# A new written-out order of steps for an attention and mixture kernel on one core: loads first, sums shared between GpSimd and VectorE

## The chip, the cores and the metric

The kernel runs on one core of one Trainium2 chip. The metric is the device time of one execution in microseconds (us); less is better. Before the change the median of three runs is 213.99 us (213.4 to 214.45).

A core has engines that run in parallel, each with its own queue that it works through strictly in order: TensorE (PE, matrix products; PEld is its weight load), VectorE (DVE), ScalarE (ACT), GpSimd (POOL) and SyncE (SP, which here only issues DMAs). An instruction at the head of a queue that waits holds up everything behind it on that engine.

## The reference

```python
scores = scale * np.matmul(x, state.transpose(0, 1, 3, 2))     # 8 batches, 8 heads, 512 tokens, 32 states, 64 deep
a = softmax(scores)                                            # over the 32 states
xread = np.matmul(a, state)
scores2 = scale * np.matmul(state, x.transpose(0, 1, 3, 2))
a2 = softmax(scores2)                                          # over the 512 tokens
sread = np.matmul(a2, x)
attn = np.concatenate([xread, sread], axis=2)                  # 544 rows a head
x = attn.transpose(0, 2, 1, 3).reshape(B * 544, 512)
h = x @ w_in                                                   # 512 to 2048
g = np.maximum(h, 0.0) + alpha * np.minimum(h, 0.0)
return g @ w_out                                               # 2048 to 512
```

`softmax` stands for the reference's three lines (subtract the maximum, exponential, divide by the sum). Inputs and output are float32; inside, the kernel works in float16 with float32 accumulation.

## The kernel before

The whole program is a list of some 1,100 short tokens, the string `ORDER`. A table `steps` maps the first part of a token to a small function, the rest are its arguments; the tokens are issued from first to last, each engine receives its instructions in that order, and the framework adds the waits that the data need. There is no scheduler behind it: the string is the schedule. An argument `a`, `v` or `p` names the engine (ScalarE, VectorE, GpSimd) where there is a choice, and a last number is the PSUM bank that a result takes.

Batches are numbered 0 to 7; "batch 8" is the block of all state rows (8 times 32). For a batch the path is:

1. Loads. `lx.b` loads a batch's tokens (GpSimd's queue, float32 cast to float16 by the DMA, line 157). Batch 0 is loaded as float32 in two halves by SyncE's queue (line 167) and cast by `cx.j.g.e` (line 173; j is the half, g the group of heads). `wi.f` and `wo.i` load quarters of `w_in` and `w_out` (lines 194 and 200), `lst` the states of batches 1 to 7 (line 188); the states of batch 0 come by ScalarE's queue as float32 and are cast by `stc` (line 237). All loads on GpSimd's queue cost GpSimd an instruction each, and stand in its order with its arithmetic.
2. Transposes. `xt`/`xo` (TensorE, and a copy out of PSUM) or `xd` (a transposing DMA) for the tokens; `stt`, `sto`, `sbd`, `str`, `sro` for the states.
3. Scores `sc`, and for batch 0 `tsc` (the scores by token, which the first softmax takes). Softmax over states: `smax`, `ssh`, `sexp`, `ssum`, `snorm`, then `at`/`ao` for batch 0 or `wb` for the others. Softmax over tokens: `tm`, `nb`, `te`, `tsum`, and `tn` (line 436), which scales the exponentials on GpSimd; then `tt` and `rd`, `rdo` for the states' reads.
4. `m.b.f` multiplies the batch's states by a quarter of `w_in`, `mo` takes the product out of PSUM. So `F.b.jc` (line 533, two matmuls of 512 columns) gets `h` for 128 of the 2048 hidden features straight from the softmax weights. `N` (line 586, ScalarE) makes the negative part and `G` (line 589, VectorE) puts `g` together. The first four features' tiles of batch 0 go in halves by `f`, `n`, `g` (lines 555, 570, 574).
5. Batches 0 and 1: `S.b.q.i` (line 603) multiplies two of the 16 feature tiles of `g` by `w_out`, `O` takes the result out. Batches 2 to 8 take a scheme with seven instead of eight products of half matrices: `U.b.i.c` (line 670) forms sums and differences of halves of `g`, each over 128 x 1024 elements (128 x 512 for batch 8), `W.i.c` (line 646) those of `w_out`, once; `P` (line 691) are the products (four matmuls of 256 columns), `K` (line 707) and `Q` (lines 722, 724) take them out. All `U` and `W` run on GpSimd.

`Z.k.n` issues n matmuls of zeros into bank k (line 220). Nothing reads them; they keep TensorE occupied while data are awaited.

In the first 30 us VectorE runs `smax.0.0` (line 363, waiting for `tsc`), the rest of batch 0's softmax, casts and copies, the first `g`, batch 1's `tm` and `sb`, then `G.0.6`, `G.0.5`; TensorE's `F` and `S` of batch 0 follow these.

Of the kernel before, what the change touches and what calls it, by code (L numbers as in the profile page):

```python
# [32 lines left out]
sc.2 tt.1 sb.2 F.1.11.0 tm.2 rdo.0.a smax.2 F.1.13.2 S.0.0.5 mo.2.2.a.1 S.0.0.7 mo.2.2.a.0 N.1.13 G.1.13 N.1.11
O.0.0.a S.0.3.0.5 G.1.11 nb.2.a te.2.1 S.0.3.7 lx.3 S.0.3.2 F.1.15.3 te.2.0 N.1.15 S.0.3.5 G.1.15 F.1.12.1 F.1.6.2
N.1.12 G.1.12 S.0.3.6 N.1.6 S.0.3.3 G.1.6 S.0.2.7 m.3.3.0.3 mo.3.3.v.1 xd.3 ssh.p.2 sexp.2 ssum.2 mo.3.3.a.0 m.3.2
mo.3.2.a F.1.14.1 W.4.0.p S.1.0.6.2 S.0.3.1 N.1.14 G.1.14 F.1.7.0 O.0.2.a N.1.7 G.1.7 S.1.0.4 F.1.3.3 N.1.3 tsum.2
S.0.3.4 S.1.0.0 m.2.3.4.1 O.0.3.a mo.2.3.v.1 mo.2.3.a.0 m.2.1 mo.2.1.a rd.1.0 m.3.0.5.4 mo.3.0.a.0 S.1.0.3 mo.3.0.a.1
S.1.0.5 sc.3 m.4.0.1.5 mo.4.0.a.0 G.1.3 mo.4.0.a.1 W.3.1.p snorm.p.2 wb.2 lx.4 S.1.3.6.3 F.2.3.4 F.2.2.1 F.2.0.5
S.1.0.7 N.2.3 sb.3 tm.3 G.2.3 rdo.1.a smax.3 N.2.2 G.2.2 N.2.0 S.1.0.1 F.2.8.0 S.1.3.7 W.4.1.p tn.2.1 tn.2.0 ssh.p.3
G.2.0 nb.3.a te.3.0 F.2.1.4 N.2.1 S.1.3.1 te.3.1 tsum.3 G.2.1 S.1.0.2 S.1.3.2 tt.2 N.2.8 G.2.8 O.1.0.a F.2.6.1 N.2.6  # L40
G.2.6 S.1.3.0 F.2.14.5 N.2.14 G.2.14 S.1.1.2.4 F.2.9.2 N.2.9 G.2.9 F.2.10.0 N.2.10 G.2.10 rd.2.1 sexp.3 ssum.3 m.3.1
F.2.5.5 mo.3.1.a F.2.11.2 S.1.3.4 S.1.3.3 S.1.2.1.0 S.1.1.3 N.2.11 G.2.11 rdo.2.a U.2.3.0.p N.2.5 xd.4 G.2.5 S.1.2.5
m.4.1.1.2 mo.4.1.a.1 sc.4 tm.4 S.1.3.5 O.1.3.a tn.3.1 F.2.4.5 tn.3.0 F.2.7.2 mo.4.1.a.0 F.2.13.3 N.2.13 lx.5 sb.4
G.2.13 S.1.1.5 tt.3 F.2.12.1 S.1.1.6 S.1.2.7 F.2.15.3 S.1.2.4 smax.4 S.1.2.3 nb.4.a te.4.0 N.2.4 N.2.7 N.2.12 G.2.4
N.2.15 S.1.2.6 S.1.2.2 S.1.1.0 G.2.7 te.4.1 S.1.2.0 O.1.2.a G.2.15 m.4.3 G.2.12 mo.4.3.a m.5.0.5.2 rd.3.3 rdo.3.a
mo.5.0.v.1 xd.5 m.4.2.1.0 mo.4.2.a.0 snorm.p.3 U.2.1.0.p U.2.2.0.p U.2.4.0.p wb.3 S.1.1.1 S.1.1.7 tsum.4 ssh.p.4
S.1.1.4 F.3.9.2 F.3.7.3 mo.5.0.v.0 sexp.4 lx.6 P.2.1.1.1.1 mo.4.2.v.1 N.3.7 O.1.1.a ssum.4 P.2.1.0.0 N.3.9 G.3.7
# [10 lines left out]
N.4.12 G.4.3 P.3.1.1.0 smax.5 F.4.14.4 K.3.1.a N.4.14 G.4.12 U.3.1.0.p U.3.2.0.p P.3.7.0.1.0 U.3.3.0.p G.4.14
P.3.7.1.1 P.3.6.0.0 F.4.15.1 N.4.15 G.4.15 P.3.6.0.1 P.3.6.1.1 N.4.10 G.4.10 P.3.6.1.0 K.3.2.a F.4.8.5 N.4.8 G.4.8
F.4.13.4 N.4.13 G.4.13 P.3.5.1.1 P.3.5.1.0 P.3.5.0.0 m.5.1 mo.5.1.a m.6.2.1.2 mo.6.2.v.0 m.7.3.5.4 mo.7.3.v.0  # L60
P.3.7.1.0 P.3.7.0.0 sc.6 mo.7.3.a.1 mo.6.2.v.1 sb.6 m.6.1.1.5 rd.4.4 mo.6.1.a.0 rdo.4.a m.7.2.2.1 mo.7.2.a.1 U.3.4.0.p
U.4.3.1.p ssh.p.5 U.4.1.0.p U.4.2.0.p smax.6 P.3.5.0.1 P.4.1.1.0.4 K.3.4.a Q.3.1.1 P.3.2.0.0.1 P.4.1.1.1 sexp.5
P.3.3.1.0 P.3.2.0.1 P.3.4.0.1 ssh.p.6 sexp.6 U.4.1.1.p U.4.2.1.p P.3.4.1.0 tm.6 mo.7.2.v.0 P.4.1.0.1 P.3.2.1.1
P.3.2.1.0 Q.3.0.0 P.4.2.0.0.2 P.4.1.0.0 K.4.1.a P.3.4.0.0 P.4.7.0.1.1 P.4.6.0.0 P.4.6.1.0 P.3.3.0.1 P.3.4.1.1
P.4.6.1.1 P.4.6.0.1 ssum.6 P.4.2.1.0 snorm.p.6 P.4.2.0.1 P.3.3.1.1 ssum.5 snorm.p.5 Q.3.1.0 K.4.2.a P.4.5.1.1
P.4.5.0.0 nb.6.a P.3.3.0.0 te.6.1 te.6.0 wb.6 F.6.3.0 wb.5 mo.6.1.a.1 Q.3.0.1.a P.4.2.1.1 P.4.5.0.1 Q.4.0.0 N.6.3
G.6.3 U.4.3.0.p F.5.8.5 N.5.8 G.5.8 tsum.6 F.5.3.3 N.5.3 F.5.2.2 N.5.2 G.5.3 lx.7 F.5.7.0 N.5.7 G.5.2 G.5.7 P.4.5.1.0
# [32 lines left out]
def kernel(  # L100
# [134 lines left out]
    def first_states_cast():  # L235
        live["st0"] = consts.tile([128, 2, D], F16, name="st0")
        nc.gpsimd.tensor_copy(live["st0"], st0_32)
# [538 lines left out]
```

## Time and profile before

| what | value |
|---|---|
| median of 3 runs | 213.99 us (213.4 to 214.45) |
| the profiled execution's own time | 213.49 us |
| its span, first to last instruction | 211.7 us |
| granted TensorE clock, mean share of full speed | 0.997 |
| first 27 us: TensorE's last wait ends | 27.11 us |
| last matmul ends | 207.9 us |
| `G` (line 589), 128x512 | 124 instructions, 85.8 us on VectorE |
| `N` (line 586), 128x512 | 124 instructions, 69.1 us on ScalarE |
| `U` (line 670), 128x1024 | 48 instructions, 2.13 us each on GpSimd |
| `tn` (line 436), 128x512 | 16 instructions, 0.69 us each on GpSimd |

The profile lists each engine's busy time, instructions grouped by source line with their mean duration, what ended an engine's idle time, and busy time within chosen stretches of the span. A busy TensorE is one with a matmul in its pipeline. "POOL 0.98" in a stretch means that GpSimd was busy for 0.98 us of it; DMA shares are the mean use of the 16 DMA engines and can pass 1, since transfers overlap.

### The profile page before, as it was taken

The page shows a single profiled execution, that of the slowest core. Times are in us where ns is not written, and L with a number is a line of the kernel's source. Part 1 is how long each engine was busy: PE and PEld are TensorE (multiplying, and loading weights), DVE is VectorE, ACT ScalarE, POOL GpSimd, SP SyncE. Part 2 cuts the span into 40 slices and gives each one's busy share as a digit, 9 for nine tenths or more (in the row PEclk, how much of TensorE's full clock was granted, in tenths as well). Part 3 has the DMA queues.
Part 4 walks back from the last instruction along what each step waited for, and adds up shares of the span by engine and source line. Part 5 has one row for each costly group of instructions (what it writes and reads, how often), then busy time and mean ns, then how long its engine had stood idle before and what let it go on. Part 6 is the DMA issues. An engine that isn't in the chain of part 4 may idle for free.

```text
span 211.7 us, 4977 instructions
## 1 busy us (share of the span) xinstructions
PE 202.8 (96%) x1979; PEld 133.1 (63%) x1979; DVE 173.0 (82%) x259; ACT 144.0 (68%) x280; POOL 182.0 (86%) x119
## 2 busy tenths in 40 slices
...
GB/s 167 159 193 206 207 196 193 88 136 143 174 144 151 170 82 168 82 3 105 60 185 3 50 62 139 116 247 37 54 99 50 104 0 0 3 96 77 89 86 151
DMA packets 52439, 23.68 MB, mean 112 GB/s; under 512 B 38465, under 2 KB 51393, under 8 KB 52417
## 3 DMA queue, kind: packets, MB, share of 16 engines
...
q8 instruction: 15, 0.25, 0.5%
...
q14 instruction: 8, 0.06, 0.1%
HBM read 17.31 MB, written 8.91 MB: 124 GB/s over the span
## 4 chain that ended last, share of the span: by engine, by line
PE 90%; DVE 5%; DMA 2%; issue 0%; ACT 0%; POOL 0%; DVEq 0%
PE h L533 25%; PE px L691 21%; PE o L603 13%; PE pv L691 11%; PE py L691 5%; PE m_ps L484 4%; PE h L542 3%; PE z L220 3%; PE sr_ps L457 2%; DMA st<-in_state_dram 2%; DVE g L574 2%; PE sc L299 1%; PE xT_ps L284 1%; PE st_ps L231 1%; DVE g L589 1%; DVE m L508 1%
## 5 line engine op out<-in xcount | busy, mean ns | idle before, releaser
L589 DVE SCALAR_TENSOR_TENSOR g<-neg,oma_sb,h 128x512 f16<-128x512 f32 (+1 forms) x140 | 92.8, 709 | 8.0 <-ACT neg L586 6.1
L586 ACT ACTIVATE neg<-h 128x512 f32<-128x512 f32 (+1 forms) x140 | 74.6, 579 | 24.7 <-PE h L533 14.7
L533 PE MATMUL h<-aT,m 128*128 128x512 f16 x248 | 66.2, 379 | 0.2 <-DVE g L589 0.2
L691 PEld LDWEIGHTS <-gsum 128*128 128x128 f16 x416 | 40.4, 98 | 9.8 <-issue 0.7
L533 PEld LDWEIGHTS <-m 128*128 128x128 f16 x248 | 23.6, 98 | 20.8 <-issue 1.9
L691 PEld LDWEIGHTS <-g 128*128 128x128 f16 x312 | 30.5, 98 | 7.8
L603 PE MATMUL o<-w_out_sb,g 128*128 128x512 f16 x128 | 33.2, 379 | 1.1 <-DVE g L574 1.1
L670 POOL TENSOR_TENSOR gsum<-g,g 128x1024 f16<-128x1024 f16 (+1 forms) x14 | 27.8, 1988 | 1.6 <-DVE g L589 0.8
L670 POOL TENSOR_TENSOR gsum<-gsum,g 128x1024 f16<-128x1024 f16 (+1 forms) x14 | 27.8, 1988 | 0.9
L670 POOL TENSOR_TENSOR gsum<-g 128x1024 f16<-128x1024 f16 (+1 forms) x14 | 27.8, 1990 | 0.3 <-DVE g L589 0.2
L670 POOL TENSOR_TENSOR gsum<-g,gsum 128x1024 f16<-128x1024 f16 (+1 forms) x14 | 27.7, 1990 | 0.3
L691 PE MATMUL px<-ws,gsum 128*128 128x256 f16 x208 | 27.1, 273 | 0.0
L603 PEld LDWEIGHTS <-g 128*128 128x128 f16 x128 | 11.9, 98 | 16.6 <-issue 1.8
L707 ACT COPY kept<-px 128x512 f32<-128x512 f32 (+1 forms) x15 | 8.4, 561 | 20.2 <-PE px L691 20.2
L385 POOL TENSOR_TENSOR an<-ts,r 128x1024 f16<-128x1024 f32 (+1 forms) x9 | 15.4, 1720 | 5.5 <-DVE r L382 4.0
L368 POOL TENSOR_TENSOR ts<-ts,mx 128x1024 f32<-128x1024 f32 x7 | 13.4, 1911 | 6.9 <-DVE mx L363 6.9
L510 ACT CAST m<-m_ps 128x512 f16<-128x512 f32 x28 | 15.6, 596 | 3.3 <-PE m_ps L484 3.1
L724 DVE TENSOR_TENSOR oq<-pv,kept 128x512 f32<-128x512 f32 (+1 forms) x14 | 9.0, 645 | 10.2 <-PE pv L691 5.7
L691 PE MATMUL pv<-ws,gsum 128*128 128x256 f16 x104 | 15.0, 273 | 0.0
L691 PE MATMUL px<-w_out_sb,g 128*128 128x256 f16 x104 | 14.8, 273 | 0.0
L691 PE MATMUL px<-w_out_sb,gsum 128*128 128x256 f16 x104 | 14.5, 273 | 0.0
L691 PE MATMUL py<-w_out_sb,g 128*128 128x256 f16 x104 | 14.5, 273 | 0.0
...
## 6 DMA issues: line engine op xcount, KB each, us to landing
...
```

Source lines behind the costliest of these rows:

```text
L368: engine(e).tensor_tensor(blocks(cols(live["ts", b], j, S)), blocks(scored(b, j)), over_blocks(cols(live["mx", b], j, S // N)), ALU.subtract,)
L385: engine(e).tensor_tensor(blocks(cols(live["an", b], j, S)), blocks(cols(live["ts", b], j, S)), over_blocks(cols(live["r1", b], j, S // N) ...
L484: nc.tensor.matmul(t[N * k : N * (k + 1), :], st_head(b, h)[64 * r : 64 * r + 64, :], w_in_sb[64 * r : 64 * r + 64, c, 512 * f : 512 * (f ...
L510: copier(e)(m_tile(b, f)[:, g, :], t[g])
L533: nc.tensor.matmul(h.rearrange("p (r j s) -> p r j s", r=2, j=2), ms[b, f][:, g, 128 * j : 128 * (j + 1)], weights(b, g), start=(g == 0), ...
L586: nc.scalar.activation(neg, h, RELU, bias=0.0, scale=-1.0)
L589: nc.vector.scalar_tensor_tensor(g_tile(b, jc), negs.pop((b, jc)), oma_sb[:, jc : jc + 1], hs.pop((b, jc)), ALU.mult, ALU.add,)
L603: nc.tensor.matmul(outs[b, q], g_tile(b, jc)[:, 128 * q : 128 * (q + 1)], w_out_sb[:, jc, :], start=not begun and jc == 2 * jc2, stop=left ...
L670: engine(e).tensor_tensor(t, x(), y(), op)
L691: nc.tensor.matmul(pbanks[b, name][:, i, :], of(b, c)[:, j, 128 * i : 128 * (i + 1)], moving[:, 4 * c + j, :], start=not begun and j == 0, ...
L707: copier(e)(t, pbanks[b, "x"])
L724: nc.vector.tensor_tensor(osb, pbanks[b, name], kept[b, add], ALU.add)
```

## The change

The order is written anew from the first token to the last. The arithmetic is the same but for the matmuls of zeros. What differs in what is issued:

| tokens | before | after |
|---|---|---|
| matmuls of zeros | 51 in 7 groups | 30 in 10 groups of 3, 18 of them ahead of everything else on TensorE |
| `stc` (first states' cast) | GpSimd | ScalarE |
| `U` on GpSimd / VectorE | 56 / 0 | 39 / 17 |
| `W` on GpSimd / VectorE | 8 / 0 | 7 / 1 |
| `tn` on GpSimd / ScalarE | 16 / 0 | 11 / 5 |
| `mo` on ScalarE / VectorE | 40 / 11 | 46 / 5 |
| `cx` on ScalarE / VectorE | 3 / 1 | 2 / 2 |
| `rdo` on ScalarE / VectorE | 8 / 0 | 5 / 3 |
| `K`, `Q`, `O` taken out by VectorE, where there is a choice | 8 | 9 |

The 18 sums that VectorE takes are, in order, W.1.0, U.2.1.1, U.3.3.0, U.4.1.1, U.6.3.1, U.6.4.0, U.6.4.1, U.7.3.1, U.7.1.1, U.7.3.0, U.7.2.0, U.8.3.1, U.7.4.1, U.8.1.1, U.8.2.0, U.8.2.1, U.8.3.0, U.8.4.1. (A `U.4.2.1` stays on GpSimd.) The code outside the order:

```diff
-    def first_states_cast():
+    def first_states_cast(e):
         live["st0"] = consts.tile([128, 2, D], F16, name="st0")
-        nc.gpsimd.tensor_copy(live["st0"], st0_32)
+        copier(e)(live["st0"], st0_32)
...
     def token_scores(j, g, k=None):
-        if g == 0:
+        if ("tsc", j) not in live:
...
-    def token_norm(b, g):
+    def token_norm(b, g, e):
         e2 = live["e2", b][:, g, :, :]
-        nc.gpsimd.tensor_scalar(
-            e2, e2, live["r2", b][:, g : g + 1], 1.0, ALU.mult, ALU.mult
-        )
+        r2 = live["r2", b][:, g : g + 1]
+        if e == "a":
+            nc.scalar.mul(e2, e2, r2)
+        else:
+            nc.gpsimd.tensor_scalar(e2, e2, r2, 1.0, ALU.mult, ALU.mult)
```

The beginning of the order, up to where batch 0's first layer is under way (the rest is rewritten in the same way):

```diff
-Z.0.9 cx.0.1.a stc stt.0 sbd.0.v Z.1.5 xt.0.0.1.1 cx.0.0.a xt.0.0.0.2 Z.3.6 sto.v cx.1.0.v sbd.1.a xt.0.1.0.3
-xo.0.0.0.v tsc.0.0.4 xo.0.0.1.a cx.1.1.a tsc.0.1 xt.0.1.1.5 smax.0.0 wi.0 xo.0.1.0.a lst ssh.v.0.0 sc.0.0 xo.0.1.1.a
-tsc.1.0.0 Z.1.2 tsc.1.1 sc.0.1 smax.0.1 ssh.v.0.1 lx.1 wi.1 sexp.0.0 wo.0 wi.2 Z.1.5 m.0.0.1.2 tm.0 wi.3 Z.3.11
-mo.0.0.a.1 ssum.0.0 str.1.3 str.0.5 mo.0.0.a.0 Z.4.13 sexp.0.1 ssum.0.1 snorm.p.0.0 at.0.4 sro.1.v xt.1.1.1.0
-xo.1.1.1.v xt.1.1.0.2 xt.1.0.1.1 snorm.p.0.1 at.1.3 nb.0.a te.0.0 te.0.1 sro.0.a m.1.0 xo.1.1.0.a ao.0.v m.2.0.5.0
-f.0.1.0.4 ao.1.a f.0.0.1.2 xt.1.0.0.3 wo.1 mo.2.0.a.1 xo.1.0.1.v mo.1.0.v oma n.0.1.0 g.0.1.0.1 wo.2 n.0.0.1
-xo.1.0.0.v m.1.1 mo.1.1.a m.0.1.1.0 f.0.1.1.3 sc.1 mo.0.1.a.0 mo.0.1.a.1 g.0.0.1.0 g.0.0.1.1 mo.2.0.a.0 f.0.0.0.2
-n.0.0.0 tsum.0 tn.0.0 F.0.5.1 n.0.1.1 g.0.1.0.0 S.0.2.1.4 N.0.5 tm.1 F.0.7.0 nb.1.a sb.1 g.0.1.1.1 F.0.6.5 te.1.1
-te.1.0 g.0.1.1.0 S.0.1.1.3 tn.0.1 g.0.0.0.0 N.0.6 g.0.0.0.1 smax.1 G.0.6 G.0.5 S.0.1.0 m.0.2 mo.0.2.a N.0.7 S.0.2.0
...
+stc.a lst Z.0.3 Z.0.3 Z.0.3 Z.0.3 Z.0.3 Z.0.3 cx.0.1.v stt.0 sto.v Z.1.3 cx.0.0.a xt.0.0.0.1 xo.0.0.0.a cx.1.1.a Z.2.3
+xt.0.0.1.2 sbd.1.v lx.1 Z.3.3 sbd.0.v tsc.0.0.3 cx.1.0.v xt.0.1.0.4 xo.0.0.1.v tsc.0.1 xt.0.1.1.5 str.0.0 xo.0.1.1.a
+Z.1.3 tsc.1.1.1 xo.0.1.0.v sc.0.1 tsc.1.0 str.1.2 sc.0.0 xt.1.0.0.4 wi.0 wi.1 smax.0.0 ssh.v.0.0 sexp.0.0 smax.0.1
+ssh.v.0.1 sro.0.a xt.1.1.0.5 sexp.0.1 xt.1.0.1.3 wo.0 xt.1.1.1.0 xo.1.0.0.a xo.1.1.1.a tm.0 nb.0.a te.0.1 wo.1
+ssum.0.1 snorm.p.0.1 sro.1.v te.0.0 m.0.0.1.4 mo.0.0.v.1 xo.1.1.0.a mo.0.0.a.0 ssum.0.0 snorm.p.0.0 at.1.0 ao.1.a
+m.2.0.2.4 m.1.0 mo.2.0.v.0 xo.1.0.1.v f.0.0.1.5 mo.1.0.a oma n.0.0.1 tsum.0 tn.0.0.p f.0.1.1.1 n.0.1.1 at.0.0 m.1.1
+mo.1.1.a m.0.1.2.3 mo.0.1.a.0 mo.0.1.a.1 g.0.0.1.0 ao.0.v f.0.0.0.0 g.0.1.1.1 g.0.1.1.0 g.0.0.1.1 sc.1 S.0.1.1.1
+F.0.7.2 mo.2.0.a.1 F.0.6.5 S.0.3.0.3 S.0.1.0 N.0.7 wi.2 f.0.1.0.4 sb.1 tm.1 N.0.6 n.0.0.0 G.0.6 nb.1.a S.0.3.1 te.1.1
+g.0.0.0.0 g.0.0.0.1 F.0.4.5 F.0.5.0 G.0.7 S.0.1.3 te.1.0 S.0.2.3.2 S.0.3.3 m.0.2 smax.1 N.0.4 S.0.2.0 G.0.4 wi.3 N.0.5
+n.0.1.0 G.0.5 S.0.3.2 g.0.1.0.1 g.0.1.0.0 W.1.0.v mo.0.2.a F.0.8.5 N.0.8 G.0.8 wo.2 wo.3 F.0.10.0 N.0.10 F.0.9.4
+G.0.10 N.0.9 G.0.9 m.0.3 mo.0.3.a S.0.2.1 F.0.11.5 S.0.2.2 S.0.1.2 F.0.14.0 ssh.p.1 sexp.1 F.0.15.4 S.0.2.4
...
```

On GpSimd the order before is: the first states' cast, then `wi.0`, `lst`, `lx.1`, `wi.1`, `wo.0`, `wi.2`, `wi.3`, then the first arithmetic. After: `lst`, `lx.1`, `wi.0`, `wi.1`, `wo.0`, `wo.1`, with nothing to wait for ahead of them; then `snorm.0.1`, `snorm.0.0`, `tn.0.0`, and behind these `wi.2`, `wi.3`, `wo.2`, `wo.3`.

More of the change, by code (lines that the diff above doesn't have):

```diff
@@ L33 @@
[L33 to L47, printed above, removed]
@@ L58 @@
[L58 to L67, printed above, removed]
@@ L73 @@
-P.5.1.0.0 m.7.1.5.3 mo.7.1.a.0 mo.7.1.a.1 sc.7 U.5.3.0.p sb.7 rd.6.4 rdo.6.a rd.5.0 rdo.5.a P.5.2.1.1.5 F.6.15.3
-N.6.15 tm.7 nb.7.a F.6.11.4 P.4.4.0.1 te.7.0 te.7.1 N.6.11 G.6.15 Q.4.1.0 P.5.2.1.0 P.5.2.0.0 tsum.7 P.5.1.0.1 K.5.1.a
-F.6.13.0 G.6.11 P.5.2.0.1 F.6.12.3 smax.7 P.5.7.0.1.1 N.6.12 G.6.12 F.6.8.4 N.6.8 U.5.1.1.p U.5.2.1.p P.5.6.1.1 N.6.13
-G.6.8 P.5.6.0.1 P.5.7.1.1 G.6.13 U.5.1.0.p U.5.2.0.p P.5.6.0.0 P.5.7.1.0 tn.7.0 ssh.p.7 sexp.7 Q.5.0.0 F.6.0.3
-P.5.6.1.0 F.6.4.4 F.6.9.0 P.5.7.0.0 tn.7.1 K.5.2.v P.5.5.1.0 ssum.7 P.5.5.0.0 N.6.0 U.5.4.0.p N.6.9 G.6.9 P.5.5.1.1
@@ new lines @@
+F.0.7.2 mo.2.0.a.1 F.0.6.5 S.0.3.0.3 S.0.1.0 N.0.7 wi.2 f.0.1.0.4 sb.1 tm.1 N.0.6 n.0.0.0 G.0.6 nb.1.a S.0.3.1 te.1.1
+g.0.0.0.0 g.0.0.0.1 F.0.4.5 F.0.5.0 G.0.7 S.0.1.3 te.1.0 S.0.2.3.2 S.0.3.3 m.0.2 smax.1 N.0.4 S.0.2.0 G.0.4 wi.3 N.0.5
+n.0.1.0 G.0.5 S.0.3.2 g.0.1.0.1 g.0.1.0.0 W.1.0.v mo.0.2.a F.0.8.5 N.0.8 G.0.8 wo.2 wo.3 F.0.10.0 N.0.10 F.0.9.4
+G.0.10 N.0.9 G.0.9 m.0.3 mo.0.3.a S.0.2.1 F.0.11.5 N.0.11 S.0.2.2 S.0.1.2 F.0.14.0 ssh.p.1 sexp.1 F.0.15.4 S.0.2.4
+N.0.14 G.0.11 S.0.3.5 tsum.1 m.1.2 ssum.1 lx.2 snorm.p.1 tn.1.1.p tn.1.0.p N.0.15 S.0.2.5 G.0.14 W.1.1.p W.2.1.p
@@ new lines @@
+te.2.1 te.2.0 F.1.0.1 N.1.0 tsum.2 S.0.0.4 G.1.1 ssh.p.2 G.1.0 sexp.2 S.0.0.6 m.3.0.4.3 m.3.2 F.1.8.0 F.1.15.1
+mo.3.2.a tn.2.0.p mo.3.0.v.0 S.0.0.2 tn.2.1.p mo.3.0.a.1 tt.2 S.1.0.1 ssum.2 N.1.8 G.1.8 F.1.12.4 N.1.12 G.1.12
+S.1.0.0 N.1.15 F.1.13.3 S.1.0.5 G.1.15 N.1.13 G.1.13 S.1.0.4 m.2.1 rd.2.0 rdo.2.v O.0.0.a mo.2.1.a m.2.3.4.1
+mo.2.3.a.1 mo.2.3.a.0 rd.1.2 m.3.3.3.0 mo.3.3.a.1 sc.3 S.1.1.0.1 S.1.1.3 snorm.p.2 W.4.0.p lx.4 wb.2 F.2.7.4 rdo.1.a
+N.2.7 F.2.8.0 N.2.8 sb.3 xd.4 S.1.1.5 F.2.2.2 smax.3 W.3.1.p ssh.p.3 mo.3.3.a.0 tm.3 S.1.0.6 S.1.0.7 O.1.0.a N.2.2
@@ new lines @@
+N.2.6 tn.3.0.p F.2.5.1 G.2.6 N.2.5 F.3.12.0 U.2.3.0.p F.3.3.3 N.3.12 U.2.1.0.p mo.4.1.a.0 N.3.3 tm.4 nb.4.a te.4.0
+S.1.3.1 S.1.3.6 U.2.2.0.p P.2.1.1.0.2 S.1.3.2 G.2.5 P.2.1.0.0 G.3.12 F.2.13.4 tt.3 lx.5 N.2.13 te.4.1 S.1.3.3 S.1.3.0
+O.1.3.a P.2.1.1.1 smax.4 G.3.3 F.3.2.1 N.3.2 m.5.2 G.2.13 m.4.2.0.5 mo.4.2.a.0 rd.3.3 rdo.3.a mo.4.2.a.1 G.3.2
+P.2.1.0.1 K.2.1.v F.3.7.4 U.2.1.1.v N.3.7 G.3.7 F.3.5.0 N.3.5 xd.5 F.3.14.1 ssh.p.4 sexp.4 P.2.2.0.0.3 tsum.4 N.3.14
+F.3.0.5 G.3.5 P.2.6.0.0 ssum.4 P.2.2.0.1 G.3.14 F.3.4.4 P.2.2.1.0 N.3.0 mo.5.2.a N.3.4 G.3.4 G.3.0 F.3.11.0 N.3.11
@@ new lines @@
+F.4.15.0 N.4.3 G.4.3 P.3.6.1.1 N.4.15 G.4.15 sexp.5 P.3.6.0.0 K.3.2.a ssum.5 m.6.1.2.5 m.5.1 mo.5.1.a P.3.7.1.0.3
+P.3.7.0.0 F.4.6.4 N.4.6 G.4.6 F.4.4.0 N.4.4 G.4.4 mo.6.1.a.0 P.3.5.0.0 P.3.5.1.0 P.3.5.1.1 P.3.5.0.1 snorm.p.5
+mo.6.1.a.1 sc.6 tm.6 m.6.2.4.2 mo.6.2.a.1 K.3.4.a m.7.3.5.0 P.3.7.0.1 P.3.7.1.1 sb.6 F.4.12.2 P.3.3.1.0 N.4.12
+P.3.3.0.0 mo.6.2.a.0 P.3.3.1.1 P.3.3.0.1 Q.3.0.1.a Q.3.1.1 P.3.4.1.1 mo.7.3.a.0 wb.5 nb.6.a G.4.12 P.3.4.0.0 U.4.1.0.p
+U.4.2.0.p U.4.1.1.v U.4.2.1.p xd.7 F.5.5.4 F.5.7.1 N.5.7 P.4.1.0.0.5 smax.6 ssh.p.6 tn.5.0.a P.3.4.0.1 P.4.2.0.0.2
```

91 lines of the change are left out of this document (52 added, 39 removed).

## The prediction

> **What bounds the kernel now.** I read the page's busy times first, then who waited on TensorE, then busy times by stretch, last the timeline of the first 28 us.
>
> ```profile
> span 211.7 us, 4977 instructions
> PE 202.8 (96%) x1979; PEld 133.1 (63%) x1979; DVE 173.0 (82%) x259; ACT 144.0 (68%) x280; POOL 182.0 (86%) x119
> ```
>
> TensorE fills 96% of the span. Its waits (total, times, longest):
>
> ```profile
> PE st_ps L231 <- POOL st L237: 1.8, 1, 1.8
> PE z L220 <- DVE zero L214: 1.3, 1, 1.3
> PE o L603 <- DVE g L574: 1.1, 1, 1.1
> PE h L555 <- DVE xT L289: 0.4, 1, 0.4
> PE h L533 <- DVE g L589: 0.2, 1, 0.2
> ```
>
> All are in the first 27.2 us. Busy us by stretch, TensorE to GpSimd:
>
> ```profile
> 30.00:80.00 50.00, 50.00 (x482) 22.18 (x481) 48.15 (x66) 43.81 (x85) 43.40 (x28) 1.00 0.94 144
> 80.00:130.00 50.00, 50.00 (x497) 36.13 (x496) 44.88 (x62) 36.51 (x69) 48.67 (x26) 1.00 0.36 79
> 130.00:180.00 50.00, 50.00 (x464) 35.32 (x463) 46.43 (x72) 35.10 (x72) 47.96 (x29) 1.00 0.39 85
> 180.00:208.00 28.00, 27.91 (x256) 24.76 (x254) 11.75 (x22) 6.01 (x15) 24.95 (x16) 1.00 0.23 76
> ```
>
> From 30 us to the last matmul TensorE never pauses, although GpSimd is at 97% from 80 to 130. So relieving GpSimd gains nothing there by itself. What can be gained lies ahead of 27 us, and what can be lost is TensorE's unbroken run. Ahead of 27 us:
>
> ```profile
> 6.61 1.17 POOL L157 DMA_DIRECT2D xg<-in_x_dram  x1
> 6.87 1.16 DVE L173 CAST xg<-x 128x512 f16<-128x512 f32 x1 [0.73 <-DMA x<-in_x_dram]
> 9.84 0.69 DVE L363 TENSOR_REDUCE mx<-tsc 128x16 f32<-128x512 f32 x1 [1.48 <-PE tsc L337]
> 14.64 1.59 PE L220 MATMUL z<-zero 128*128 128x256 f16 x13
> 19.40 0.48 DVE L574 SCALAR_TENSOR_TENSOR g<-neg,oma_sb,h 128x256 f16<-128x256 f32 x1
> 26.33 0.73 DVE L589 SCALAR_TENSOR_TENSOR g<-neg,oma_sb,h 128x512 f16<-128x512 f32 x1
> 27.11 0.59 PE L533 MATMUL h<-aT,m 128*128 128x512 f16 x2 [0.21 <-DVE g L589]
> ```
>
> VectorE starts the softmax at 9.84, works almost without a gap, ends `G.0.6` at 27.06, and TensorE's last wait is for it (27.11). So the end is set by when VectorE reaches `G.0.6`; behind it TensorE runs 180.8 us to 207.9, and 3.8 us follow for the last copy and store. I compare where the new order has VectorE at points with the same work behind.
>
> **The change, part by part.**
>
> *Work ahead of G.0.6.* By the two orders TensorE has the same real work in front of `G.0.6` but for two tokens each way (`F.0.5`, `S.0.2.1` against `S.0.3.0`, `S.0.1.0`), each two matmuls of 512 columns. So at `G.0.6` what is left is the same, and an earlier `G.0.6` moves the end one for one.
>
> *Zero matmuls.* Of 51, 30 stay. The first nine took 2.10 us, 0.23 each; 18 take 4.2, from 1.33 to 5.5, and the first states' transposes began at 5.19: at most 0.3 late, hidden behind batch 0's tokens, which landed at 5.36 and 6.87. The other 12 (0.12 to 0.24 each, 1.4 to 2.9) stand where TensorE waits for copies. The 13 at 14.64, which reached past the first `an`, are gone. Price zero: VectorE's queue covers them; without that cover, at most 2.9 lost.
>
> *States' cast.* On GpSimd 0.29 at 4.85; on ScalarE the nearest copy took 0.37 (line 249), and ScalarE was idle until 5.36. Zero, bounds -0.1 to 0.3.
>
> *Loads at once.* GpSimd's first load was issued at 5.09, behind that cast; now `lst` and `lx.1` go out at about 1.3, as soon as the identity is made, and `wi.0`, `wi.1`, `wo.0`, `wo.1` follow at 0.55 to 1.2 each. Nothing at 27 us waited for them, so the gain is nil; the cost is that they share the DMA engines with batch 0's tokens, which had these alone:
>
> ```profile
> 3.00:4.00 1.00, 0.43 (x3) 0.00 (x0) 0.00 (x0) 0.00 (x0) 0.00 (x0) 1.00 0.94 267
> 5.00:6.00 1.00, 0.81 (x7) 0.52 (x8) 0.34 (x2) 0.64 (x2) 1.00 (x2) 1.00 1.20 294
> 8.00:9.00 1.00, 1.00 (x6) 0.61 (x5) 0.36 (x2) 0.58 (x2) 1.00 (x2) 1.00 1.28 196
> ```
>
> The last columns are DMA share and GB/s written. GpSimd's loads write 196 GB/s, thus read 392 as they cast. `wi.0`, issued at 5.09, shows in the DMA rate about two us later, so `lst` should flow from 3, when about 0.88 MB of the tokens' 1.05 is still to come. If both share evenly, 0.88 MB of reads go between: 0.88/0.39 = 2.2 us, the second half lands at 9.1 instead of 6.87. Bounds: no delay (6.9); all of `lst` and `lx.1` first, 0.74 MB written at 200 GB/s, 3.7 us (10.5). I take 9.1, for the shares stand near the full 16 engines already.
>
> *From the tokens to the softmax.* VectorE then does `cx.1.0` and two transposes' copies before `smax.0.0`. The cast took 1.16 on VectorE while GpSimd issued a load (6.61 to 7.78; it ended 0.25 after it), 0.62 on ScalarE. GpSimd's issues are over by about 6.5 now, so 0.6 (bounds 0.3 to 1.16), two copies 0.42 each, 0.15 for TensorE's score: start at 10.7, against 9.84.
>
> *From the softmax to G.0.6.* Start-to-start steps of VectorE: four halves of `smax`/`ssh` 2.71, `tm` 1.13, `ssum` 0.86, `sro` 1.08, `mo` 0.62, `ssum` 0.86, `mo` 0.62, `xo` 0.36, two small ones 0.27: 8.5. Next is `g.0.0.1.0`, which needs ScalarE: from 1.4 after the start 0.64 `sexp`, 1.06 `sro`, 0.64, two `xo` 1.18, 0.2, `te` 1.76, `xo` 0.59, `mo` 0.60, `ao` 0.59, `mo.1.0` 1.0, `n` 0.62, less some 0.06 overlap each: 9.6. So VectorE waits 1.1. Then four `g` and an `ao` 1.96, `sb` and `tm` 2.29, `G.0.6` 0.67: 14.5 after the start, 25.2. Before it was 17.2 after its start (two more `mo`, `xo` and four more `g` and `smax.1` stood ahead). Lead: 27.06 - 25.2 = 1.9 us.
>
> *The next tight point* is `F.0.11`, whose bank `G.0.8` frees: 0.80 `g`, 0.67, `smax.1` 1.13, 1.34, 0.80, `W.1.0` 0.7, 0.67, thus 20.6 after the start, 31.3. TensorE has 12 more `F` and `S` (0.432) and two `m` (0.28) behind it there, 5.7 us, than before at `G.0.5` (27.7): 33.4 by before's pace. Lead 2.1, so `G.0.6` decides.
>
> *wi.2 and wi.3* now wait on GpSimd behind `snorm` and `tn`: issued at about 20.1 and 20.9. An unqueued quarter lands in 5.8, the next 2.5 later: 25.9 and 28.5. `m.0.3` is due at about 29.6. Zero, with 1 us to spare; its cover gone, one for one.
>
> *Sums on VectorE.* Twelve of 128x1024 and six of half that: 15 full ones. No row before has VectorE in such a sum. Float16 copies (0.272 for 256, 0.416 for 512) grow 0.56 ns an element: 0.70. Float32 ones (0.424, 0.69): 1.22. The other moves (six `mo` off, `rdo`, `Q`, `cx` on) come to about -1. VectorE's total: 173 - 1 + 15 x 0.7 = 182; at 1.22, 190. Four full ones fall before about 130 us, where VectorE idles 7.0 of the 100 us from 30; eleven later, where it idles 19.8 of 78. Below 1.7 each they are hidden there; I take 0.7, as it is nearest in type, and price zero, with one exception counted above (`W.1.0`).
>
> The clearest case against it is GpSimd's own work: if a VectorE sum must wait for a running one, it waits up to 2.13. The Trainium skill, page "SBUF — State Buffer", section "Who interferes with whom", says that a VectorE instruction with two SBUF inputs contends with a GpSimd one that reads SBUF, and that the later blocks for the whole of the other. The cast above, which ended just behind GpSimd's issue, looks like such a block; of sums no run here shows it yet.
>
> *tn on ScalarE*, 0.69 on GpSimd, at most that on ScalarE, which is at 68%: zero.
>
> **Sum.** -1.9 from `G.0.6`, +0.1 for the 0.3 of first transposes that may show: -1.8. The profiled execution was 213.49, so 211.7; the median is 0.5 above it: 212.2.
>
> **Rivals.**
>
> 1. Tokens hardly delayed (7.5): softmax at 9.1, lead 3.5, the median 210.5. For it: shares above 1 show transfers overlapping. Against: both streams read at 300 to 390 GB/s alone.
> 2. Tokens delayed to the bound, 10.5: softmax at 12.1, lead 0.5, thus no change, 213.5. For it: `lx.1` is cut into pieces as small as the tokens'.
> 3. Slower: VectorE's sums wait for GpSimd's. GpSimd falls to about 146 us busy (69%), a mean wait of 0.69 x 1.07 = 0.73, a sum then 1.4, still hidden. At 2.1 each, four cost 8.4 against 7.0 and eleven 23.1 against 19.8: 4.7 lost, less 1.8: +2.9, 216.9. It decides from about 1.9 each. For it: GpSimd's sums stand back to back, and `G`'s of the next tiles queue behind a waiting sum. Against: after 180 us VectorE is 42% busy, and half of the sums fall near there.
>
> **How the numbers follow.** Forecast 0.37 (own range 211.2 to 213.0), rival 1 0.11, rival 2 0.22, rival 3 0.30 with worse delays of the start in it. What a measurement here can tell from no change is about 0.5%, 1.1 us. Faster 0.47, same 0.22, slower 0.31. The range reaches from rival 1 to rival 3: 210.2 to 217.0.
>
> **What would show it.** Right: the tokens' second cast at 8.5 to 9.5, `smax.0.0` at 10 to 11.3, `G.0.6` done by 25.5, no TensorE wait beyond 0.3 after 32 us, `U` on VectorE near 0.7. Wrong: TensorE waits on line 592's `g` between 30 and 150, `U` on VectorE above 1.7, or `m.0.3` waiting for `wi.3`.

## The result, and the profile after

Each kernel was run 18 times, in turn on one chip. The kernel before took 213.56 us (median; 212.88 to 214.45), the changed one 216.45 us (214.35 to 218.1): ratio 1.011, 95% interval 1.0082 to 1.0138. The change makes the kernel 1.1% slower; forecast was 212.2. The ratios leave out executions more than 1.5% above the fastest of their kernel and are not quotients of the medians (that would be 1.0135 here).

The runs of the changed kernel fall into two groups, 7 from 214.35 to 215.42 and 11 from 216.12 to 218.1. The profiled execution took 217.11 and belongs to the second. Its span and busy times, from the page (engine, busy us, share, instructions):

```profile
span 215.3 us, 4942 instructions
PE 204.7 (95%) x1958; PEld 132.3 (61%) x1958; DVE 180.8 (84%) x276; ACT 148.2 (69%) x287; POOL 147.9 (69%) x95
```

GpSimd lost 34 us of work and VectorE gained 8, as intended and as forecast (182 and "about 146"). The time is elsewhere. The waits of TensorE (engine, what waited, what for; total us, times, longest):

```profile
PE sr_ps L460 <- DMA e2T<-e: 1.8, 1, 1.8
PE at_ps L350 <- POOL an L386: 1.7, 1, 1.7
PE z L221 <- DVE zero L215: 1.3, 1, 1.3
PE m_ps L487 <- ACT xT L290: 0.6, 1, 0.6
PE sc L300 <- ACT m L511: 0.4, 1, 0.4
PE h L536 <- DVE g L577: 0.2, 1, 0.2
```

The first line is new: that wait ends at 59.8 us, where TensorE never paused before. No line names a sum. Busy us by stretch, in the columns of the prediction:

```profile
15.00:20.00 5.00, 2.74 (x33) 0.99 (x32) 4.91 (x9) 4.68 (x12) 1.72 (x2) 0.81 1.24 206
30.00:80.00 50.00, 48.04 (x435) 20.89 (x434) 45.27 (x64) 42.86 (x81) 36.23 (x24) 1.00 0.80 135
80.00:130.00 50.00, 49.95 (x512) 34.13 (x511) 47.05 (x67) 41.67 (x81) 46.90 (x26) 1.00 0.72 118
130.00:180.00 50.00, 50.00 (x487) 36.73 (x485) 46.58 (x73) 36.49 (x75) 43.40 (x23) 1.00 0.23 62
```

From 30 to 80 us 1.96 of TensorE's time is missing; from 80 on it is as full as before, although VectorE now does the sums.

To place the loss I use one curve below: at a point of the trace, the time so far less the real matmuls done so far, each at its undisturbed pace of the trace before (0.2155 us for 512 columns, 0.109 for 256). Both kernels do 189.9 us of such work; the rest is "lost".

| lost by | 28 us | 45 us | 58 us | 60 us | 100 us | the last matmul |
|---|---|---|---|---|---|---|
| before | 15.48 | 16.06 | 16.40 | 16.40 | 16.86 | 17.82 |
| after | 16.43 | 17.51 | 17.87 | 19.96 | 20.70 | 21.42 |

Of 3.6 us, 0.95 are lost by 28 us, 0.5 more by 45 (what takes these was not traced), and 2.1 between 58 and 60; 1.8 of these 2.1 are the wait that ends at 59.8.

The start, in order of time (start, duration, engine, line, what, how many):

```profile
2.59 3.83 PE L221 MATMUL z<-zero 128*128 128x256 f16 x13
6.57 0.42 PE L232 MATMUL st_ps<-ident,st 128*64 128x128 f16 x4
6.92 0.82 PE L221 MATMUL z<-zero 128*128 128x256 f16 x3
```

The states had been cast at 4.87. TensorE still worked through its 18 matmuls of zeros until 6.4, so the first transposes came at 6.57 (before 5.19), and between the next ones stood groups of three zeros at 0.82 to 0.84 each. VectorE, the same way:

```profile
5.07 0.43 DVE L174 CAST xg<-x 128x512 f16<-128x512 f32 x1 [3.80 <-DMA x<-in_x_dram]
7.85 0.41 DVE L174 CAST xg<-x 128x512 f16<-128x512 f32 x1
11.54 0.68 DVE L364 TENSOR_REDUCE mx<-tsc 128x16 f32<-128x512 f32 x1
25.99 0.73 DVE L592 SCALAR_TENSOR_TENSOR g<-neg,oma_sb,h 128x512 f16<-128x512 f32 x1
```

The second line stands behind other VectorE work, not behind a landing: the tokens had landed at 7.5. `smax.0.0` starts at 11.54 (before 9.84). `G.0.6` ends at 26.72 (before 27.06). TensorE's last wait of the start is no longer for it but for the `g` right behind it on VectorE (line 577), 0.20 us, and ends at 27.56 (before 27.11).

The point at 59.8: SyncE's list first, then TensorE.

```profile
54.64 1.61 SPq L277 DMA_TRANSPOSE xT<-xg  x1
56.42 1.30 SPq L445 DMA_TRANSPOSE e2T<-e  x1
```

```profile
59.76 0.68 PE L460 MATMUL sr_ps<-e2T,xg 128*64 128x32 f16 x32 [1.78 <-DMA e2T<-e]
```

`rd.2` on TensorE needs what `tt.2` transposes (second line, issued at 56.42, landed at 59.6). `tt.2` stands on SyncE behind `xd.3` (first line), and `xd.3` waits for `lx.3`, which GpSimd issues at 46.8, only after `rd.0` has freed a buffer. In the order before, `rd.2` came on TensorE at about 65 us, 7 us later than it was due here (58).

### The profile page after: what moved, and what is told of

Its sections match the earlier page's. It is cut to its first block, busy times and chain, and to the rows that moved or that the text cites. A ratio compares the mean times of both kernels' runs of the same rounds, so it can differ in the third digit from the quotient of the medians.

```text
span 215.3 us, 4942 instructions
## 1 busy us (share of the span) xinstructions
PE 204.7 (95%) x1958; PEld 132.3 (61%) x1958; DVE 180.8 (84%) x276; ACT 148.2 (69%) x287; POOL 147.9 (69%) x95
## 4 chain that ended last, share of the span: by engine, by line
PE 87%; DVE 6%; DMA 3%; issue 1%; ACT 1%; POOL 0%; SPq 0%; POOLq 0%
PE h L536 23%; PE px L694 21%; PE pv L694 11%; PE o L606 10%; PE py L694 5%; PE m_ps L487 4%; PE z L221 3%; PE h L545 3%; PE sr_ps L460 2%; DMA xT<-xg 2%; DMA e2T<-e 1%; DVE g L592 1%; DVE nb L406 1%; PE sc L300 1%; DVE mx L364 1%; PE h L558 1%
## 5 line engine op out<-in xcount | busy, mean ns | idle before, releaser
L536 PE MATMUL h<-aT,m 128*128 128x512 f16 x248 | 67.3, 379 | 0.2 <-DVE g L577 0.2
L673 POOL TENSOR_TENSOR gsum<-gsum,g 128x1024 f16<-128x1024 f16 x11 | 23.4, 2126 | 17.8 <-DVE gsum L673 17.1
L694 PE MATMUL px<-ws,gsum 128*128 128x256 f16 x208 | 28.1, 273 | 0.0
L673 POOL TENSOR_TENSOR gsum<-g,g 128x1024 f16<-128x1024 f16 (+1 forms) x10 | 21.1, 2113 | 3.2 <-PE px L694 2.7
L673 POOL TENSOR_TENSOR gsum<-g,gsum 128x1024 f16<-128x1024 f16 (+1 forms) x10 | 20.3, 2035 | 3.6 <-PE px L694 2.1
L513 ACT CAST m<-m_ps 128x512 f16<-128x512 f32 x33 | 18.5, 606 | 3.4 <-PE m_ps L487 3.2
L673 POOL TENSOR_TENSOR gsum<-g 128x1024 f16<-128x1024 f16 x8 | 17.0, 2130 | 1.8 <-DVE g L592 1.8
L694 PE MATMUL py<-w_out_sb,g 128*128 128x256 f16 x104 | 15.4, 273 | 0.0
L511 ACT CAST m<-m_ps 128x1024 f16<-128x1024 f32 x13 | 13.3, 1023 | 1.7 <-PE m_ps L487 1.5
L694 PE MATMUL pv<-ws,g 128*128 128x256 f16 x104 | 14.0, 273 | 0.0
```

The costliest lines, as they stand in the source:

```text
L511: copier(e)(m_tile(b, f), t)
L513: copier(e)(m_tile(b, f)[:, g, :], t[g])
L536: nc.tensor.matmul(h.rearrange("p (r j s) -> p r j s", r=2, j=2), ms[b, f][:, g, 128 * j : 128 * (j + 1)], weights(b, g), start=(g == 0), ...
L673: engine(e).tensor_tensor(t, x(), y(), op)
L694: nc.tensor.matmul(pbanks[b, name][:, i, :], of(b, c)[:, j, 128 * i : 128 * (i + 1)], moving[:, 4 * c + j, :], start=not begun and j == 0, ...
```

## The experiments

All ratios are to the kernel before, run on the same chip in the same turn (its medians there: 213.6 to 213.9), with 95% intervals; a gain in us is the difference of two ratios by 213.6. Edits are shown as moves in the order. In runs with one and the same beginning TensorE comes to its full pace early or late, for no reason that the runs show (last section), which shifts the loss by 28 us by 1.6 to 2.0; so single traces are compared at the start only with that in mind, and the medians decide.

**The sums.** All 18 back on GpSimd, the rest as changed:

```diff
-W.1.0.v U.2.1.1.v U.3.3.0.v U.4.1.1.v ...
+W.1.0.p U.2.1.1.p U.3.3.0.p U.4.1.1.p ...
```

> The changed kernel with all 18 sums of VectorE back on GpSimd, places unchanged. Theory C (the sums are hidden either way up to the end, 0.69 us each on VectorE): up to 170 us no difference; behind it the products wait for GpSimd's sums of batches 6 to 8, 2.13 us each, so 1 to 6 us slower. Rival (VectorE's sums take the slack that TensorE lives on): 0.5 us or more faster.

Measured 233.8 us (232.58 to 234.63), ratio 1.0948 (1.0898 to 1.0998). TensorE's waits:

```profile
PE px L693 <- POOL gsum L672: 10.6, 5, 4.0
```

In this order the sums on VectorE are worth nearly 18 us, far more than the 1 to 6 that were expected: the order counts on them. And in the changed kernel no wait of TensorE names one, so they are no part of the loss that shows.

**The start: zeros.** The changed kernel without the nine zeros between the transposes:

```diff
-cx.1.1.a Z.2.3 xt.0.0.1.2 sbd.1.v lx.1 Z.3.3 sbd.0.v
+cx.1.1.a xt.0.0.1.2 sbd.1.v lx.1 sbd.0.v
```

(and `Z.1.3` behind `sto.v`)

> The changed kernel without the nine zero matmuls (three groups of 3) that stand between the first transposes; the 18 ahead and the last 3 stay. Theory B (the zeros stand on the chain to the first maximum, at 0.27 us each): the first maximum starts at about 9.5 to 10 instead of 11.5, and the end moves up by 1 to 1.7 us, 214.8 to 215.5. Rival (TensorE gets slower without them, or the copies behind the tokens' landing decide): the first maximum stays after 11 and the time within 0.4 us.

Measured 214.85 us (213.8 to 217.4), ratio 1.0052 (1.0024 to 1.0079). `smax.0.0` began at 9.40 instead of 11.54; lost by 28 us: 15.45 instead of 16.43, both with the late pace.

Nine instead of eighteen zeros ahead, those between kept:

```diff
-stc.a lst Z.0.3 Z.0.3 Z.0.3 Z.0.3 Z.0.3 Z.0.3 cx.0.1.v
+stc.a lst Z.0.3 Z.0.3 Z.0.3 cx.0.1.v
```

> The changed kernel with nine instead of eighteen zero matmuls ahead of the first transposes (three groups of three taken out). Queue theory: eighteen held TensorE until 6.4 us while the states had been cast at 4.9; with nine, the states' transposes start at about 5.1 instead of 6.57, the first softmax comes up to 1.4 us earlier (10.2 instead of 11.5) and the time falls by about 1 to 215.4. Rival: the zeros are what warms TensorE, the transposes then run slower by as much, the first softmax comes no earlier than 11.2 and the time stays.

Measured 214.8 us (213.29 to 216.43), ratio 1.0037 (1.001 to 1.0063); states' transposes at 5.28, `smax.0.0` at 9.82, lost by 28 us 14.12 (in an execution whose granted clock stayed at 1.00; see the gap below). Either group of zeros, priced at nothing in the prediction, costs time: by the ratios 1.2 us for those between and 1.6 for nine of those ahead. TensorE's queue at the start is on the path, and VectorE's first softmax follows it.

The zeros of the kernel before are another matter. That kernel with its first nine alone:

```diff
-sbd.0.v Z.1.5 xt.0.0.1.1 ... Z.3.6 ... Z.1.2 ... Z.1.5 ... Z.3.11 ... Z.4.13 sexp.0.1
+sbd.0.v xt.0.0.1.1 ... sexp.0.1
```

> The kernel before with its first nine zero matmuls alone; the 42 others (five groups between transposes and scores, one of 13 ahead of at.1.0) are left out. They change no value. Clock theory: they stand where TensorE waits anyway, without them its clock falls in 10 to 20 us as it does in the changed kernel, and the time is 0.4 to 1.0 longer than 213.8. Rival: zeros between real matmuls are in the way here as in the changed kernel, and it is 0.5 to 1.5 shorter.

Measured 214.14 us (213.64 to 214.86), ratio 1.0011 (0.9994 to 1.0027). Neither theory: the 42 zeros are worth nothing that can be told. The eight `f` matmuls became slower (1.62 against 1.05 us).

**The start: loads at once.** The kernel before with `stc` on ScalarE and `lst`, `lx.1` first:

```diff
-Z.0.9 cx.0.1.a stc stt.0 ... wi.0 xo.0.1.0.a lst ssh.v.0.0 ... smax.0.1 ssh.v.0.1 lx.1 wi.1
+stc.a lst lx.1 Z.0.9 cx.0.1.a stt.0 ... wi.0 xo.0.1.0.a ssh.v.0.0 ... smax.0.1 ssh.v.0.1 wi.1
```

> The kernel before with one part of the change alone: the first states' cast on ScalarE, and lst and lx.1 as GpSimd's first loads. Prediction's theory (the loads share the DMA engines with batch 0's tokens): the second half of the tokens lands at 9 instead of 6.9, the first maximum moves from 9.8 to 10.5 or later, 0.5 to 1.5 us slower, 214.1 to 215. Rival (tokens are not delayed, as the trace of the changed kernel suggests: their last large packets went at about 6 us): within 0.4 us of before, 213.2 to 214.

Measured 216.12 us (215.14 to 217.02), ratio 1.0118 (1.0071 to 1.0164): 2.5 us slower, more than either theory gives. In the profiled execution the second half of the tokens was cast at 7.23 and 8.15 (before 6.87 and 7.96), `smax.0.0` began at 10.45 (before 9.84), and the new wait of TensorE is

```profile
PE m_ps L483 <- DMA w_in_sb<-in_moe_w_in_dram: 1.3, 1, 1.3
```

`wi.0`, now the third load of the queue instead of the first; `m.0.0` came at 14.04 instead of 11.96. So the early loads delay the load behind them by far more than batch 0's tokens. A part may be the clock: it was granted at 0.91 and 0.74 in the two stretches from 10 to 20 us here, and the four executions fall into two at a mean clock of 0.992 (216.95, 217.02) and two at 0.997 and 1.00 (215.14, 215.3). In the changed kernel the late `wi.0` does not show, since its `m.0.0` comes later.

**SyncE's list.** My first idea of the wait at `rd.2` was that `tn.0.1`, moved to ScalarE, holds up SyncE (it waits there until 40.19 for `tt.0`, and everything behind comes later). The changed kernel with it on GpSimd again:

```diff
-tn.0.0.p ... tn.0.1.a N.0.12 tt.0
+tn.0.0.p tn.0.1.p ... N.0.12 tt.0
```

> The changed kernel with one token moved: tn.0.1 goes to GpSimd, right behind tn.0.0, instead of to ScalarE much later. Theory A (SyncE's queue): the transposing DMA of batch 0's scaled exponentials no longer waits for ScalarE until 40.2 us, batch 2's tokens are transposed as soon as they have landed (about 38.5 instead of 41.7), everything behind them on SyncE moves up, and TensorE's wait of 1.8 us for the exponentials of batch 2 before line 460 goes: 1.5 to 2.5 us faster than the changed kernel, 214 to 215. Rival (the transposing DMAs are slow by themselves, 3 to 5 us, among the other transfers): the wait stays, 216 to 217.

Measured 216.77 us (214.59 to 217.42), ratio 1.0131 (1.0074 to 1.0188), and the wait at `rd.2` still took 1.4: this idea fell. `xd.3` was issued at 54.13 instead of 54.64, since it waits for `lx.3`, which comes from `rd.0`. Next, the two transposing loads exchanged:

```diff
-xd.3 G.1.11 ... tt.2 S.1.0.1
+G.1.11 ... tt.2 xd.3 S.1.0.1
```

> The changed kernel with one place moved: on SyncE's list xd.3 (the transposing load of batch 3's tokens, which waits for GpSimd's lx.3) stands behind tt.2 (the transposing load of batch 2's routing weights) instead of 43 places ahead of it. Queue theory: rd.2 on TensorE waited 1.78 us at 59.8 for tt.2's data, and tt.2 stood on SyncE behind a waiting xd.3; with it ahead, tt.2 is issued some 2 us earlier, the wait goes, and the time falls by 1.5 to 2 to 214.5 to 215. Rival: xd.3 issued later makes sc.3 the next wait, or the loss comes back elsewhere, and the time stays at 216.0 to 216.8.

Measured 214.27 us (213.03 to 215.87), ratio 1.0026 (0.9991 to 1.006). SyncE's list in that run:

```profile
52.19 1.24 SPq L444 DMA_TRANSPOSE e2T<-e  x1
53.53 1.66 SPq L276 DMA_TRANSPOSE xT<-xg  x1
```

`tt.2` goes out 4.2 us earlier (1.8 of it because this execution is ahead: `tt.0` went out at 38.40, in the changed kernel at 40.19), the wait at `rd.2` is gone, TensorE waits for nothing between 30 and 208 us, and `xd.3` behind it delays no one. Its times form two groups as well, 213.03 to 213.94 and 214.6 to 215.87, each some 1.5 below that of the changed kernel. By the ratios this one place is worth 1.8 us, of which some 0.3 is that more of its executions fell into the faster group, and with it moved no difference that can be told remains between the kernels.

**The gap ahead of `at`.** Where the kernel before has 13 zeros the changed one waits 1.7 us for GpSimd's `an`, the granted clock is 0.81 there, and the eight `f` matmuls behind took 1.89 us (before 1.05). With 13 zeros put there:

```diff
-ssum.0.0 snorm.p.0.0 at.1.0 ao.1.a
+ssum.0.0 snorm.p.0.0 Z.0.13 at.1.0 ao.1.a
```

> The changed kernel with 13 zero matmuls put back ahead of at.1.0, where the kernel before had them and the changed one waits 1.7 us for GpSimd's an. Nothing is removed. Clock theory: TensorE stands still in that wait, and its granted clock of 0.81 to 0.85 from 15 to 25 us comes from it; with the gap filled the clock there goes back to about 1, the 8 f matmuls of L558 (1.89 us) come back to about 1.05, and the time falls by 0.4 to 0.8. Rival: the clock is set by something else, the zeros only stand in line, and the time is the same or 0.3 to 0.6 longer.

Measured 218.86 us (217.1 to 219.51), ratio 1.0243 (1.0201 to 1.0285). The clock was 1.00 and the eight `f` took 1.03, as the clock theory says; lost by 28 us was 13.94, against 14.80 in a run of like pace (the one before). And yet the ratio rose by 1.3%, 2.8 us. In the profiled execution, the fastest of the four, all that was won at the start, and more, was lost again at transposing loads, 1.6 at `sc.2`, 0.85 at `rd.2` and 2.3 at `rd.4`:

```profile
PE sr_ps L459 <- DMA e2T<-e: 3.1, 2, 2.3
PE sc L299 <- DMA xT<-xg: 1.6, 1, 1.6
```

Is that SyncE's list again? The same with `xd.3` behind `tt.2`:

> The changed kernel with xd.3 behind tt.2 on SyncE's list and 13 zeros ahead of at.1.0, the two edits that were run one by one before (214.27 and 218.86). The zeros in the gap made the start 0.9 us quicker in the trace (14.80 to 13.94 us lost at 28 us) and TensorE then waited 1.6, 0.85 and 2.3 us for transposing loads. Queue theory: those waits come from the places on SyncE's list, the second one (rd.2) goes with xd.3's move, and since the whole order then runs without the delay that made xd.5 and tt.4 late, the others shrink too: 213.0 to 214.0. Rival: an earlier start meets the loads of sc.2 and rd.4 as before, and it stays above 215.5.

Measured 217.26 us (216.69 to 217.75), ratio 1.0141 (1.0106 to 1.0176). The exchange gains here too, 2.2 us by the ratios, but the rival held: the wait at `rd.2` went, that of `sc.2` stayed, 2.2 us, since `xd.2` took 5.9 us from issue to landing (3.8 in the changed kernel). Right behind it on SyncE's queue stands an output store, some packets of which took up to 1.7 us in this trace. With that store moved:

```diff
-xd.2 N.1.4 G.1.4 O.0.1.a ... tt.1 F.1.10.1
+xd.2 N.1.4 G.1.4 ... tt.1 O.0.1.a F.1.10.1
```

> The run with xd.3 behind tt.2 and the 13 zeros in the gap (217.26), with one place more moved: the output's store O.0.1 (with ScalarE's copy for it) stands behind tt.1 on SyncE instead of between xd.2 and tt.1. Store theory: in that run TensorE waited 2.2 us at sc.2 for xd.2's data, which took 5.9 us from issue to landing against 3.8 elsewhere, and right behind it on SyncE's queue stood this store, some of whose 2 KB packets took up to 1.7 us; with the store later xd.2 lands in about 3.8, the wait goes and the time falls by about 2 to 215.0 to 215.5. Rival: the late landing has another cause than the store, the wait stays above 1.5 us and the time above 216.7.

Measured 217.2 us (215.31 to 221.0), ratio 1.0134 (1.0084 to 1.0184). `xd.2` still took 5.5 us; TensorE waited 0.5 at `sc.2`, 1.2 for ScalarE's late copy of that output, and 2.2 at `rd.4`. The store is not the cause.

The traces hold another candidate. The page counts 15 packets of 16 KB of the kind "instruction" in an execution; with 3,916 instructions of TensorE that is one for about 260 of them. In these three traces such a packet is moved while `xd.2` is under way, at 42.0, 44.4 and 41.7, and `xd.2` takes 5.3, 5.9 and 5.5 us. In the other nine traces of the new order it comes only after `xd.2` has landed (44.1 to 46.3), and `xd.2` takes 3.6 to 3.9. It is the same with `tt.4`, which `rd.4` waits for: 5.9, 4.3 and 5.9 us with a packet, 3.1 in the nine without. These three kernels issue 43 matmuls of zeros, the nine others at most 30, so the program's own loading would come earlier in the work. No run moves such a packet alone: that it holds the transposing loads fits all twelve traces, and is not shown.

The clock theory is not whole either. Low clock and slow `f` together stand in all five profiles with eighteen zeros ahead and the gap left empty, and in no other. With nine zeros ahead the 1.7 us wait was there just the same, but the granted clock of the profile stayed at 1.00 and the `f` took 1.03. That profile is not the usual case, though: over a whole execution the changed kernel's mean clock is 0.981 to 0.992, and with nine zeros ahead it was 0.989 to 0.992 in eight executions of ten (214.53 to 216.43 us) and 1.00 in two, the profiled one and the fastest (214.15 and 213.29). A mean does not tell where in an execution the clock was low. So the same order gets the lower clock or not from one execution to the next; what decides it I can't say.

**All together.** `xd.3` behind `tt.2`, the 13 zeros in the gap, nine zeros ahead, none between, `str.0.0` behind the tokens' transposes:

```diff
-stc.a lst Z.0.3 Z.0.3 Z.0.3 Z.0.3 Z.0.3 Z.0.3 cx.0.1.v stt.0 sto.v Z.1.3 cx.0.0.a ... tsc.1.0 str.1.2
+stc.a lst Z.0.3 Z.0.3 Z.0.3 cx.0.1.v stt.0 sto.v cx.0.0.a ... tsc.1.0 str.0.0 str.1.2
```

> The changed kernel with the edits of the other three runs together, and without the zero matmuls between the transposes: xd.3 behind tt.2, 13 zeros in the gap ahead of at.1.0, nine zeros ahead, none between, and the states' first projection str.0.0 behind the tokens' transposes tsc.1.0. If the losses are where the traces put them (2.1 at the start, 0.5 in the gap, 1.8 at rd.2), it comes out at 211.5 to 213, ahead of the kernel before (213.56). Rival: the gains overlap, since VectorE's queue, not TensorE's start, sets when the experts' work can begin, and it stays at 213.5 to 215.

Measured 213.02 us (212.57 to 213.76), ratio 0.9971 (0.995 to 0.9992): 0.3% ahead of the kernel before and, by the two ratios, 1.4% ahead of the changed one. No wait after 30 us; lost by 28 us 14.20, at the last matmul 16.88. The gain of 3.0 us is 1.6 short of the sum of the single ones (1.8, 1.2, 1.6; the zeros in the gap, a loss of 2.8 by themselves, are not in it), so the rival is partly right: VectorE has no pause longer than 0.7 us from 12.7 to 30 us in that trace, and an earlier TensorE gives little there.

Without its 13 zeros:

> The run with all edits together (213.02) without its 13 zeros ahead of at.1.0; the 1.7 us wait there is then empty again. Clock theory: the granted clock falls below 0.9 from 15 to 20 us and the time is 0.4 to 1.0 longer, 213.4 to 214.0. Rival: behind VectorE's queue, which has no pause from 12.7 us on in that run, the clock of this stretch costs nothing, and it is 212.6 to 213.2.

Measured 214.03 us (212.86 to 215.45), ratio 0.9998 (0.997 to 1.0026). The intervals overlap; the zeros in the gap are worth 0.6 us here by the ratios, which is not clear of noise. The granted clock was 1.00 without them in the profiled execution, but that is the fastest of the ten, and in five others the mean clock was 0.990 to 0.992 (213.47 to 214.05 us). With the gap filled, in the run before and the next one, it was 0.996 or more in all 22 executions. So the zeros go with the higher clock, as the clock theory says; what that is worth stays open, since three executions without them took 214.56 to 215.45 at a mean of 1.00. With twelve instead of nine ahead, and the 13 in the gap again:

> The run with all edits together (213.02) with twelve zero matmuls ahead instead of nine, so that TensorE is busy without a pause from 1.3 us until the states' cast lands at about 5. Theory of an early full rate: work without a pause is what lets TensorE reach its full rate at 6.4 us instead of about 10, as in some executions with eighteen zeros; the first transposes then run at full rate in a part of the executions and the time is 212.2 to 212.8. Rival: VectorE's queue sets the start from 12.7 us on, and it stays at 212.9 to 213.3.

Measured 213.22 us (212.16 to 213.54), ratio 0.997 (0.9952 to 0.9988). The rival holds: no gain over nine.

## Why the prediction was wrong, step by step

- **The bound.** "From 30 us to the last matmul TensorE never pauses" was read rightly, and so was what follows from it, that the change can lose TensorE's unbroken run. The step that failed is that only VectorE's and GpSimd's queues were then searched for that loss. SyncE's list was not looked at, although its order is rewritten too: `xd.3` ahead of `tt.2`, and `rd.2` 7 us sooner. The run with the two loads exchanged gives 1.8 us for this, of the 4.2 between forecast and result.
- **Zero matmuls, "price zero: VectorE's queue covers them".** This is the other mis-sized term: 0.3 and at most 2.9 were written, and the cover was taken for granted. In the first 11 us VectorE waits for TensorE (1.45 and 1.07 us ahead of its two copies of `xo`), so there is no cover. 18 zeros took 5.09 us, not 4.2: a group of three takes 0.85, not three times 0.23. Taking away either group gave 1.2 to 1.6.
- **Loads at once, second half of the tokens "at 9.1".** Wrong in cause: the second half landed 6.3 us after its issue at 1.25, at 7.5, in the kernel before at 6.8. In both traces 97% of the tokens' packets are done by 6.1 us, the last one at 6.5 before and 7.2 after. GpSimd's first load, issued at 1.44, shows its first packets at 5.3 us, 3.9 later; in the trace before that took 1.7 (5.09 to 6.8). So the loads hardly met the tokens. Rival 1's premise, 7.5, was thus right, and its time was not, since the zeros took the place of the delay: the start of the softmax came at 11.54, behind the 10.7 forecast and near rival 2's 12.1.
- **Cast on VectorE, 0.6.** 0.41 to 0.43. The 1.16 of before was read as a possible block by GpSimd's load issue. Here the cast at 5.07 ran in 0.43 while GpSimd was issuing two loads (4.85 to 6.54), so an issue alone does not hold it up.
- **From the softmax to `G.0.6`, 14.5.** 15.2 (11.54 to 26.72); the `f` matmuls of 1.89 us lie in it. The lead of 1.9 shrank to 0.35, and TensorE's last wait, now for the `g` behind `G.0.6`, ended 0.45 later than before. Nor does "an earlier `G.0.6` moves the end one for one" hold: with all edits together `G.0.6` ended at 24.06, 3.0 us before that of the kernel before, and the last matmul at 206.97, 0.9 before; behind `G.0.6` 182.9 us went by, in the kernel before 180.9. So a lead at `G.0.6` is worth less than itself here; what takes the other 2 us was not traced. In the run with the exchanged loads, which begins alike but with the early pace, 14.80 were lost by 28 us, 0.7 less than before: so of the gain of 1.8 that was forecast for the start, 0.7 was there in one execution and -0.95 in the other.
- **wi.2, wi.3, states' cast: zero.** Held. TensorE waits for no weights.
- **Sums, 0.70 each and hidden.** The price held: of the 11 `U` of 128x1024 ten took 0.68 to 0.69 and one 1.75. Rival 3's price of 2.1 each did not come. The Trainium skill, page "SBUF — State Buffer", section "Who interferes with whom", has a VectorE instruction with two SBUF inputs contend with a GpSimd one that reads SBUF. In this trace a hold can be seen at two of the 17 `U`, one of each size, and TensorE waited for neither. The time lay near rival 3's 216.9 all the same, by other causes; its agreement with the result is chance.
- **`tn` on ScalarE, zero.** `tt.0` did wait for it until 40.19, but moving it back gained nothing.
- **The sum.** Forecast -1.8, result +2.9. The lead that was to give -1.9 became a loss of 0.95 by 28 us and 1.45 by 45 in the profiled execution; the 2.1 around 59.8 us were not in the sum at all.
